# Linear attention beside softmax attention on one core: a transposing load held back, a copy split in two, the flag read earlier

## The chip, the core and the metric

The kernel runs on one core of one Trainium2 chip. The core has five engines with queues of their own: TensorE (PE, matrix products), VectorE (DVE), ScalarE (ACT), GpSimd (POOL) and SyncE (SP, which here only issues DMAs). Each works through its instructions in the order in which the program has them and waits on semaphores for the others. The metric is the device time of one execution in microseconds (us).

## The reference

Two attention blocks on inputs of their own, their results laid side by side. x is 1 x 2048 x 512, wqkv 512 x 1536, wo 512 x 512, all bfloat16; there are 32 heads of 16.

```python
def _A_ref(x, wqkv, wo):                      # linear attention
    q, k, v = qkv[0], qkv[1], qkv[2]          # qkv = x @ wqkv, split into heads
    phi = lambda t: jnp.where(t > 0, t + 1, jnp.exp(t)) + 1e-6
    pq, pk = phi(q), phi(k)
    kv = jnp.einsum("bhsd,bhse->bhde", pk, v)
    z = jnp.einsum("bhsd->bhd", pk)
    num = jnp.einsum("bhqd,bhde->bhqe", pq, kv)
    den = jnp.einsum("bhqd,bhd->bhq", pq, z)[..., None] + 1e-6
    o = num / den
    return (heads of o side by side) @ wo

def _B_ref(x, wqkv, wo):                      # softmax attention
    scores = jnp.einsum("bhqd,bhkd->bhqk", q, k) * Dh ** -0.5
    p = _softmax(scores, axis=-1)
    o = jnp.einsum("bhqk,bhkd->bhqd", p, v)
    return (heads of o side by side) @ wo

return jnp.concatenate([a, b], axis=-1)
```

Block B needs 32 x 2048 x 2048 exponentials, and these fill most of the time.

## The kernel before

**The work of B.** The 32 heads form four groups of eight, a group's 128 columns of Q and K being the 128 partitions of a tile. A unit of work is one group, 512 queries and one parity of heads; there are 32 units. Within a unit a block is 128 keys for one head: a matmul on 32 of TensorE's rows (L862) with the key tile KM, in which the other head of the 32 rows has been zeroed (L1366, L605), against the query tile QT. The scores lie in PSUM: five banks named pS, two of which or three are one ScalarE instruction (1024 or 1536 columns, L1074, to the tile PT), and two banks named pD for VectorE and GpSimd, which compute the exponential by integer arithmetic on the bits of a float16 (L978, L1148, tile DI). TensorE then multiplies by V, which carries a column of ones for the softmax sum (L1222, PSUM tile pPV). ScalarE's slots alternate: three banks, two banks, three banks.

**The order of the work.** The program plans itself while it is built: a loop keeps a time for each engine, a list of candidates and the times at which inputs are expected, and always takes the next candidate by its costs. What it takes becomes the fixed order of instructions of each engine. Work of block A, projections and outputs are jobs that are fitted in between. The planner begins only after a start that is written out by hand, with the engines' times and the due times of x's tiles set as constants. Semaphore waits follow from the reads and writes that each operation declares (`sch.add(lane, fn, reads, writes, queue=..., extra_deps=...)`); the first argument is the engine, or a DMA lane with a semaphore of its own, and `queue` is the engine that issues the DMA.

**The start.** B's x is wanted transposed, as the tile xTb with 16 tiles of 128 rows of x. Tiles 2 and 3 are loaded plainly (tile ON, ScalarE's queue) and transposed by TensorE (L1346); all others come by transposing DMAs on SP's queue (`load_t`, L443): tiles 0 and 1, 4 to 7, 8 to 11, 12 to 15. The weights are the tile Wb: ScalarE's queue loads the first 128 columns of K's and of Q's (keys ("Wb", 1, 0) and ("Wb", 0, 0)), SP's queue those of V (key ("Wb", 2)) behind tiles 4 to 7, and later the rest; A's x and weights (xTa, Wa) follow on SP. Then:

- `warm(n)` (L1335) issues n matmuls of 128 columns on a tile of zeros. WARM = (30, 8): 30 before the transposes of L1346, 8 behind them.
- `first_mm` (L1358) projects K of tile 0 (bank k0), Q of tiles 0 and 1 (q0), Q of tiles 2 and 3 (q1), K of tile 1 (k1), K of tiles 2 and 3 (k2). `first_ev` copies them to KM and QT: K by VectorE, twice with a mask; q0 by ScalarE (L1368), q1 by VectorE (L1370).
- The first five scores (L862) fill ScalarE's two slots. They wait for QT's pieces, keys ("QT0", 0) and ("QT0", 1).
- The planner's first jobs follow on TensorE in this order: K's projection for tiles 4 to 7 (L591), three scores for ScalarE's third exponential, V's projection (L668), two scores for the fourth exponential, V's projection again, and so on; K's projection for tiles 8 to 11 (L591) comes some rounds later.

**The end.** Four last stores go to the output (L1327). An operation "final" on GpSimd waits for the last store of every lane. Because the exponential is computed without subtracting the row's maximum, a bound on the scores is computed on the way (FLG); at the end each engine reads FLG into a register (L1594) and branches (L1596): where the bound is over a threshold, a general version of B runs instead. `emit_queue` writes an engine's instructions and calls `hook`, which holds this read, once it comes to an operation behind a given index, after that operation's waits. For GpSimd that operation is "final"; the other engines reach the end of their list and read there.

Of the kernel before, what the change touches and what calls it, by code (L numbers as in the profile page):

```python
# [238 lines left out]
def bass_concat_heads__linear_attn_block__softmax_full_mha__prompt_kernel(nc, A_x, A_wqkv, A_wo, B_x, B_wqkv, B_wo, out):  # L239
# [106 lines left out]
    DSH = 0.5  # L346
    FM = 0.06
    JB = True
    WARM = (30, 8)
    TRACE = None  # L350


# [3 lines left out]
    sch = Sched()  # L356
    es = contextlib.ExitStack()
    with es:
        block = es.enter_context(nc.Block())

        def sb(name, shape, dt):
            return es.enter_context(nc.sbuf_tensor(name, shape, dt))
# [4 lines left out]
        xTb = sb("xTb", [128, 4, S], BF)  # L367
        xTa = sb("xTa", [128, 2, 4, 512], BF)
        Wb = sb("Wb", [128, 4, 1536], BF)
        Wa = sb("Wa", [128, 4, 1536], BF)  # L370
        WOa, WOb = Wa[:, :, 512:1024], Wa[:, :, 1024:1536]
        QT = sb("QT", [128, 2, S], BF)
# [38 lines left out]
        def bank(T, b0, key):  # L411
            return (T, T.bitcast(BF), b0 * 512, key)
        DBANK = [bank(DB, i, ("D", i)) for i in range(NB)]
        SBANKS = [bank(S5, i, k_) for i, k_ in enumerate((("S", 0, 0), ("S", 0, 1), ("S", 0, 2), ("S", 1, 0), ("S", 1, 1)))]
# [10 lines left out]
        def gapped(ap, c0, n, run):  # L425

            base = ap[:, c0:c0 + run]
            return bass.AP(base.tensor, base.offset, [list(base.ap[0]), [run + 1, n], [1, run]])


        def load(dst_ap, src_ap, writes, queue="sp"):
            lane = sch.new_dma_lane()
            sch.add(lane, lambda e: e.dma_start(dst_ap, src_ap), writes=writes, queue=queue)
# [3 lines left out]
        on_keys = lambda k: [("ON", k, g) for g in range(8)] + ([("xTb", t) for t in range(4 * (k - 12), 4 * (k - 12) + 4)] if k >= 12 else [])  # L437
        on_at = lambda k: ONL[:, k, :] if k < 12 else xTb[:, 0, (k - 12) * 512:(k - 11) * 512]

        def load_t(dst, dname, x, t0, n):  # L440

            lane = sch.new_dma_lane()
            sch.add(lane, lambda e: e.dma_start_transpose(dst[:, :, t0 * 128:(t0 + n) * 128], x[0][t0 * 128:(t0 + n) * 128, :]),  # L443
                    writes=[(dname, t) for t in range(t0, t0 + n)], queue="sp")
        load(ONL[:, 2:4, :], B_x[0].rearrange("(t p) c -> p t c", p=128)[:, 2:4, :], on_keys(2) + on_keys(3), queue="act")
        load_t(xTb, "xTb", B_x, 0, 2)
        load(Wb[:, :, 512:640], wbv[:, :, 512:640], [("Wb", 1, 0)], queue="act")
        load(Wb[:, :, 0:128], wbv[:, :, 0:128], [("Wb", 0, 0)], queue="act")
        load_t(xTb, "xTb", B_x, 4, 4)
        load(Wb[:, :, 1024:1536], wbv[:, :, 1024:1536], [("Wb", 2)])  # L450
        load_t(xTb, "xTb", B_x, 8, 4)
        load_t(xTb, "xTb", B_x, 12, 4)
        load(Wb[:, :, 128:512], wbv[:, :, 128:512], [("Wb", 0, g) for g in range(1, NGP)])
# [76 lines left out]
        def push(eng, ready, prio, dur, run):  # L530
            seq[0] += 1
            c_ = (ready, prio, seq[0], dur, run)
            cands[eng].append(c_)
            return c_
# [282 lines left out]
        def unit(u):  # L817
            Gp, r2 = divmod(u, NC * 2)
            return (Gp,) + divmod(r2, 2)
# [45 lines left out]
        def qk_reads(bl):  # L865
            res = []
            for u, j, g in bl:
                Gp, c, e_ = unit(u)
                res += [("QT", Gp % 2, c), ("KMj", e_, j, g) if Gp % 2 == 0 and j < 4 else ("KM", Gp % 2, e_, j // 4, g)]
                if Gp == c == 0:  # L870
                    res += [("QT0", i) for i in range(2)]
            return res

        held = [False] * (NB + 1)
# [85 lines left out]
        def d_emit(tk, en):  # L960

            for b, buf, bi in tk:
                bk = DBANK[bi]
                sch.add("pe", lambda e, bk=bk, b=b: qk(e, f32v(bk), b), reads=qk_reads([b]), writes=[bk[3]])
            for b, buf, bi in tk:
                def p1(st_, en_, buf=buf, bi=bi):
                    bis = [bi]
                    for b2 in (bi + 1, bi - 1):
                        o = waiting.get(b2) if bi < NB and b2 < NB else None
                        if o is not None and o[0] == buf and o[2][0] <= st_ + 0.02:  # L970
                            cands["dve"].remove(o[2])
                            bis = sorted((bi, b2))
                            T["dve"] = en_ = st_ + 0.065 + 0.535 * 2
                            break
                    n, b0 = len(bis), bis[0]
                    s_ = dgroup["st"][buf]
                    i = len(s_["items"])
                    sch.add("dve", lambda e: e.tensor_scalar(DI[:, buf, D0_ + i * 512:D0_ + (i + n) * 512], f32v(DBANK[b0], n * 512),  # L978
                                                             ESC, EB, op0=ALU.mult, op1=ALU.add),
                            reads=[DBANK[x][3] for x in bis], writes=[("DI", 0, buf, i + x) for x in range(n)])  # L980
                    for x in bis:
                        b_ = waiting.pop(x)[1]
                        k_ = len(s_["items"])
                        s_["items"].append(b_)
                        dfree[x] = en_ + LPE["dve"]
                        pv_ready[b_[0]].append((en_ + LPE["dve"], b_, (DI.bitcast(F16)[:, buf, D0_ + k_ * 512:D0_ + (k_ + 1) * 512], ("DI", 0, buf, k_)), ("d", buf), "V"))
                    s_["t"] = en_
                    chain(buf)
                waiting[bi] = (buf, b, push("dve", en + LAT, 0, 0.6, p1))
# [16 lines left out]
        def fill_act_cand():  # L1006
# [24 lines left out]
            def run(st, en):  # L1031
# [28 lines left out]
                def f(e):  # L1060
                    for i, b in enumerate(bl):
                        ins = qk(e, S5[:, c0 + i * 512:c0 + (i + 1) * 512], b)
                    return ins
                sch.add("pe", f, reads=qk_reads(bl), writes=skeys(sl, len(bl)))
                if tk:
                    d_emit(tk, en + 0.05)
# [265 lines left out]
        def warm(n):  # L1332
            def f(e):
                for i_ in range(n):
                    ins = e.matmul(f32v(DBANK[0], 128), lhsT=ZW[:], rhs=ZW[:], start=True, stop=True)  # L1335
                return ins
            sch.add("pe", f, reads=["ZW"], writes=[DBANK[0][3]], accum="warm")
        warm(WARM[0])
        tok["Wb2"] = 10.9
# [3 lines left out]
        for t, bk, lane in ((2, SBANKS[1], "dve"), (3, SBANKS[2], "act")):  # L1343
            def tr(e, t=t, bk=bk):
# [6 lines left out]
                reads=[bk[3]], writes=[("xTb", t)])  # L1351
        warm(WARM[1])
        q0, q1, k0, k1, k2 = SBANKS[0], SBANKS[3], DBANK[2] if NB > 2 else SBANKS[4], DBANK[0], DBANK[1]

        def first_mm(bk, kind, t0, n, c0):
            def f(e):
                for cc in range(4):
                    ins = e.matmul(bk[0][:, bk[2] + c0:bk[2] + c0 + n * 128], lhsT=Wb[:, cc, kind * 512:kind * 512 + 128],  # L1358
                                   rhs=xTb[:, cc, t0 * 128:(t0 + n) * 128], start=(cc == 0), stop=(cc == 3))
                return ins  # L1360
            sch.add("pe", f, reads=[("Wb", kind, 0)] + [("xTb", t) for t in range(t0, t0 + n)], writes=[bk[3]])

        def first_ev(lane, bk, keys, dst, c0, n, wr, e_=None):
            src = bk[0][:, bk[2] + c0:bk[2] + c0 + n]
            if e_ is not None:
                sch.add(lane, lambda e: e.tensor_scalar(dst, src, PAR[:, e_:e_ + 1], None, op0=ALU.mult), reads=keys + [("PAR", e_)], writes=wr)  # L1366
            elif lane == "act":
                sch.add(lane, lambda e: e.activation(dst, src, ACTF.Copy), reads=keys, writes=wr)  # L1368
            else:
                sch.add(lane, lambda e: e.tensor_copy(dst, src), reads=keys, writes=wr)  # L1370
# [4 lines left out]
        for e_ in range(2):  # L1375
            first_ev("dve", k0, [k0[3]], KM[:, 0, e_, 0:128], 0, 128, kj(e_, [0]), e_)
        first_ev("act", q0, [q0[3]], QT[:, 0, 0:256], 0, 256, [("QT0", 0)])
        first_mm(q1, 0, 2, 2, 0)
        first_ev("dve", q1, [q1[3]], QT[:, 0, 256:512], 0, 256, [("QT0", 1)])
        first_mm(k1, 1, 1, 1, 0)  # L1380
        for e_ in range(2):
            first_ev("dve", k1, [k1[3]], KM[:, 0, e_, 128:256], 0, 128, kj(e_, [1]), e_)
# [108 lines left out]
        while True:  # L1491
# [5 lines left out]
            for eng in T:  # L1497
                best = None
                for c_ in cands[eng]:
                    st = max(T[eng], c_[0])  # L1500
                    k_ = (round(st / 0.05), c_[1], c_[2])
# [27 lines left out]
            t0 = min(o[0] for o in opts)  # L1529
# [41 lines left out]
        last = {}  # L1571
        for s_ in stores:
            last[s_.lane] = s_
        sch.add("pool", lambda e: None, extra_deps=list(last.values()), name="final")

        flag_op = sch.last_write["FLG"]
# [2 lines left out]
        sems = {ln: es.enter_context(nc.semaphore("s_" + ln)) for ln in sch.lane_ops.keys()}  # L1579
# [10 lines left out]
        def run(queue, e):  # L1590
            got = []
            def hook(e):
                e.wait_ge(sems[flag_op.lane], flag_op.count)
                got.append(e.value_load(FLG.bitcast(mybir.dt.int32)[0:1, 0:1], min_val=0))  # L1594
            sch.emit_queue(queue, e, sems, hook=(len(sch.ops) - 2, hook))
            with e.If(got[0] > THRESHOLD_BITS):  # L1596
                for ln, tot in totals.items():
                    if tot:
                        e.wait_ge(sems[ln], tot)
                gsch.emit_queue(queue, e, gsems)  # L1600
# [49 lines left out]
```

## Time and profile before

| what | us |
|---|---|
| median of 3 runs | 663.15 (663.01 to 664.05) |
| the profiled execution | 663.59 |
| its span, first to last instruction | 661.9 |
| ScalarE busy | 646.1 (98%) |
| TensorE busy | 635.4 (96%) |
| VectorE busy | 632.9 (96%) |
| GpSimd busy | 589.5 (89%) |

Rows of a timeline read: start in us, duration in us, engine, line, operation, output<-input, shapes, how many in a row; in brackets the engine's idle time before it and what ended it. PEld is TensorE's weight load ahead of a matmul, SPq and ACTq are the queues of SP and ScalarE with the DMAs that they issue. A row of DMA issues has the kilobytes of one and the us from its issue to its landing; where a stretch has only one such DMA, that is its own. A row of a DMA queue has packets, MB and the share of time of the 16 DMA engines. A row of one line's instructions has shortest, median and longest duration in ns and the first and last start in us.

### The profile page before, as it was taken

What the parts mean: (1) busy time and instruction counts of PE and PEld (TensorE: products, weight loads), DVE (VectorE), ACT (ScalarE), POOL (GpSimd) and SP (SyncE); (2) the same over time, 40 slices, a digit from 0 to 9 for tenths busy, and PEclk for the clock granted to TensorE, in tenths of its full rate; (3) what the DMA queues carried; (4) which work ended last, traced back from release to release, by engine and by line L of the source; (5) the groups of instructions that cost most, each with busy time, mean ns of one, the idle gap of its engine ahead of it and who ended that gap; (6) DMA issues with size and microseconds to landing.
All of it is one profiled execution on the core that took longest, in us unless ns stands there. A gap on an engine that the chain in (4) does not pass through costs nothing.

```text
span 661.9 us, 15921 instructions
## 1 busy us (share of the span) xinstructions
PE 635.4 (96%) x6603; PEld 201.5 (30%) x6658; DVE 632.9 (96%) x1065; ACT 646.1 (98%) x691; POOL 589.5 (89%) x493
## 2 busy tenths in 40 slices
PE   9999999999999999999999999999999999999996
PEld 6323332323323333323222223222222233222222
DVE  4999999999999999999999999999999999999985
ACT  6999999999999999999999999999999999999994
POOL 5989999998999998899989999899999999999981
PEclk9999999999999999999999999999999999999999
DMA  9701011010101101301002011100011000111011
GB/s 179 205 2 20 13 10 33 9 42 9 33 2 33 33 2 33 72 26 33 17 19 49 9 34 34 25 10 15 11 34 33 9 1 3 25 33 41 17 42 53
DMA packets 53214, 21.54 MB, mean 33 GB/s; under 512 B 44176, under 2 KB 52624, under 8 KB 53136
## 3 DMA queue, kind: packets, MB, share of 16 engines
q1 hardware_dynamic: 51664, 19.80, 13.4%
q8 instruction: 54, 0.88, 0.6%
q10 hardware_dynamic: 1472, 0.66, 0.4%
q14 instruction: 24, 0.20, 0.1%
HBM read 4.46 MB, written 4.19 MB: 13 GB/s over the span
## 4 chain that ended last, share of the span: by engine, by line
ACT 94%; PE 4%; DVE 1%; issue 0%; DMA 0%; DVEq 0%
ACT PT L1074 91%; ACT EA L684 2%; PE pD L800 1%; PE pPV L1222 1%; PE pS L862 1%; PE pD L1335 1%; DVE DI L978 0%; DMA out_dram<-KNa 0%; PE pS L1358 0%; DVE KNa L573 0%; PE pS L1274 0%; DVE DI L1154 0%; PE pS L800 0%; PE pS L1346 0%; PE pD L650 0%
## 5 line engine op out<-in xcount | busy, mean ns | idle before, releaser
L1074 ACT ACTIVATE PT<-pS 128x1024 f16<-128x1024 f32 (+1 forms) x653 | 639.0, 1312 | 1.0 <-PE pS L862 1.0
L1148 POOL TENSOR_SCALAR DI<-DI 128x1024 int16<-128x1024 int16 (+1 forms) x412 | 551.4, 1338 | 47.9 <-DVE DI L978 20.8
L978 DVE TENSOR_SCALAR DI<-pD 128x512 int16<-128x512 f32 (+1 forms) x463 | 324.5, 715 | 7.3 <-PE pD L862 3.9
L862 PE MATMUL pS<-QT,KM 32*128 32x512 bf16 x1555 | 256.8, 384 | 8.6 <-ACT PT L1074 3.4
L1222 PE MATMUL pPV<-PT,VV 128*17 128x512 f16 x1372 | 229.0, 381 | 0.0
L1222 PE MATMUL pPV<-DI,VV 128*17 128x512 f16 x1352 | 219.2, 381 | 0.2 <-DVE OT L1251 0.2
L862 PE MATMUL pD<-QT,KM 32*128 32x512 bf16 x493 | 168.7, 384 | 0.1
L1222 PE MATMUL pPV<-DI,VX 128*17 128x512 f16 x676 | 153.1, 384 | 0.0
L862 PEld LDWEIGHTS pS<-QT,KM 32*128 32x128 bf16 x1555 | 64.8, 90 | 263.7 <-ACT PT L1074 228.8
L978 DVE TENSOR_SCALAR DI<-pS 128x512 int16<-128x512 f32 x183 | 124.2, 679 | 1.1 <-PE pS L862 0.4
L1132 DVE TENSOR_SCALAR DI<-DI 128x1056 int16<-128x1056 int16 x118 | 80.6, 689 | 0.4
L1222 PEld LDWEIGHTS pPV<-PT,VV 128*17 128x17 bf16 x1372 | 47.7, 88 | 43.6 <-issue 37.8
L1222 PEld LDWEIGHTS pPV<-DI,VV 128*17 128x17 bf16 x1352 | 46.3, 88 | 40.6 <-issue 32.1
L862 PEld LDWEIGHTS pD<-QT,KM 32*128 32x128 bf16 x493 | 40.0, 91 | 5.2 <-DVE DI L978 2.5
L1222 PEld LDWEIGHTS pPV<-DI,VX 128*17 128x17 bf16 x676 | 32.8, 88 | 20.4 <-issue 17.0
L709 PE MATMUL pD<-Wa,xTa 128*128 128x256 bf16 x192 | 29.3, 275 | 0.0
L591 PE MATMUL pD<-xTb,Wb 128*128 128x512 bf16 x81 | 25.3, 382 | 3.3 <-issue 2.8
L1251 DVE STREAM_TRANSPOSE OT<-pPV 128x512 f32<-128x512 f32 x31 | 21.9, 707 | 0.1
L1257 POOL TENSOR_TENSOR OT<-OT,ZR 128x256 bf16<-128x256 f32 x31 | 19.2, 620 | 2.3 <-DVE ZR L1256 0.9
L684 ACT ACTIVATE EA<-pD 128x512 bf16<-128x512 f32 x22 | 18.6, 847 | 0.0
L709 PEld LDWEIGHTS pD<-Wa,xTa 128*128 128x128 bf16 x192 | 14.8, 97 | 12.5 <-issue 5.9
L573 DVE CAST KNa<-pD 128x512 bf16<-128x512 f32 x23 | 15.7, 682 | 2.1 <-PE pD L800 1.9
(145 smaller groups left out, 352.0 us busy)
## 6 DMA issues: line engine op xcount, KB each, us to landing
out_dram<-KNa SPq DMA_DIRECT2D x31, 128.0 KB, 1.7
Wa<-in_A_wqkv_dram SPq DMA_DIRECT2D x1, 1536.0 KB, 8.3
KM<-KR SPq DMA_DIRECT2D x96, 16.0 KB, 1.8
Wb<-in_B_wqkv_dram SPq DMA_DIRECT2D x2, 384.0 KB, 4.2
Wb<-in_B_wqkv_dram SPq DMA_DIRECT2D x1, 512.0 KB, 4.9
Wa<-in_A_wo_dram SPq DMA_DIRECT2D x1, 512.0 KB, 3.8
Wa<-in_B_wo_dram SPq DMA_DIRECT2D x1, 512.0 KB, 3.8
ON<-in_B_x_dram ACTq DMA_DIRECT2D x1, 256.0 KB, 2.8
```

What stands on the lines that cost most here:

```text
L573: return lambda e, bk: (e.tensor_copy(out_fn(), in_fn(bk)) if lane == "dve" else e.activation(out_fn(), in_fn(bk), ACTF.Copy))
L591: return e.matmul(f32v(bk), lhsT=Wb[:, cc, kind * 512 + Gp * 128:kind * 512 + Gp * 128 + 128], rhs=xTb[:, cc, sc * 512:(sc + 1) * 512], st ...
L684: ("act", 0.052 + n * 0.000833, f_ev("act", lambda e, bk: e.activation(EA[:, 0:n], f32v(bk)[:, c0:c0 + n], ACTF.Exp), [], ["EA"])),
L709: return e.matmul(f32v(bk)[:, 256 * tt:256 * tt + 256], lhsT=xTa[:, b, cc, (o + tt) * 128:(o + tt + 1) * 128], rhs=Wa[:, cc, 512 * kind + ...
L862: return e.matmul(dst, lhsT=KM[32 * g:32 * g + 32, Gp % 2, e_, j * 128:(j + 1) * 128], rhs=QT[32 * g:32 * g + 32, Gp % 2, c * 512:(c + 1) ...
L978: sch.add("dve", lambda e: e.tensor_scalar(DI[:, buf, D0_ + i * 512:D0_ + (i + n) * 512], f32v(DBANK[b0], n * 512), ESC, EB, op0=ALU.mult, ...
L1074: sch.add("act", lambda e: e.activation(PTf[:, p0 * 512:p0 * 512 + w], S5[:, c0:c0 + w], ACTF.Exp, scale=SC), reads=skeys(sl, len(bl)), wr ...
L1132: sch.add("dve", lambda e: e.tensor_scalar(gapped(DI[:, buf, :], DIV[v], wide // 32, 32), DI[:, buf, D0_ - 32:D0_ + w], 1.0, float(SHIFT[v ...
L1148: sch.add("pool", lambda e: e.tensor_scalar(DI[:, sl, DIV[v]:DIV[v] + w], DI[:, sl, D0_:D0_ + w], 1.0, float(SHIFT[v - 1]), op0=ALU.mult, ...
L1222: sch.add("pe", lambda e, g=g, j=j, c0=c0, V_=V_, r2=r2, P=P, first=first, last_=last_: e.matmul(PVb[32 * g:32 * g + 17, 0:512] if len(P.s ...
L1251: sch.add("dve", lambda e: e.transpose(OT[:, 0, :], PVb[:, 0:512]), reads=[("PV", g) for g in range(4)], writes=[("OT", 0)])
L1257: ("pool", 0.7, f_op("pool", lambda e: e.tensor_tensor(xn[:, :, 16 * e_:16 * e_ + 16], o[:, :, 0:16], zr.unsqueeze(2).broadcast_to([128, 1 ...
```

## The change

- `load_t` takes a list of keys, and the DMA for tiles 4 to 7 waits until ("Wb", 0, 0), Q's first 128 columns of weights, has landed. The wait stands in SP's queue.
- The 8 matmuls of the second `warm` become 4.
- The projection of Q for tiles 2 and 3 becomes two, each with a bank of its own and 128 columns: VectorE copies tile 2's, ScalarE tile 3's. The first scores wait for three pieces of QT instead of two.
- An operation "mark" on GpSimd, which does nothing, stands ahead of "final", and `hook` is set to come ahead of it. GpSimd so reads FLG before it waits for the stores; the branch stays behind that wait. The other engines read it where they did.

The planner's constants stay as they are, and so does the order of everything behind the first projections.

```diff
-    WARM = (30, 8)
+    WARM = (30, 4)
...
-        def load_t(dst, dname, x, t0, n):
+        def load_t(dst, dname, x, t0, n, after=()):
 
             lane = sch.new_dma_lane()
             sch.add(lane, lambda e: e.dma_start_transpose(dst[:, :, t0 * 128:(t0 + n) * 128], x[0][t0 * 128:(t0 + n) * 128, :]),
-                    writes=[(dname, t) for t in range(t0, t0 + n)], queue="sp")
+                    writes=[(dname, t) for t in range(t0, t0 + n)], queue="sp", extra_deps=[sch.last_write[k_] for k_ in after])
...
-        load_t(xTb, "xTb", B_x, 4, 4)
+        load_t(xTb, "xTb", B_x, 4, 4, [("Wb", 0, 0)])
...
-                    res += [("QT0", i) for i in range(2)]
+                    res += [("QT0", i) for i in range(3)]
...
-        first_mm(q1, 0, 2, 2, 0)
-        first_ev("dve", q1, [q1[3]], QT[:, 0, 256:512], 0, 256, [("QT0", 1)])
+        q2 = SBANKS[1]
+        first_mm(q1, 0, 2, 1, 0)
+        first_mm(q2, 0, 3, 1, 0)
+        first_ev("dve", q1, [q1[3]], QT[:, 0, 256:384], 0, 128, [("QT0", 1)])
+        first_ev("act", q2, [q2[3]], QT[:, 0, 384:512], 0, 128, [("QT0", 2)])
...
+        mark = sch.add("pool", lambda e: None, name="mark")
         sch.add("pool", lambda e: None, extra_deps=list(last.values()), name="final")
...
-            sch.emit_queue(queue, e, sems, hook=(len(sch.ops) - 2, hook))
+            sch.emit_queue(queue, e, sems, hook=(mark.idx - 1, hook))
```

## The prediction

> **What bounds the kernel now.** I read the page first: the chain that ended last, then the costliest groups.
>
> ```profile
> ACT 94%; PE 4%; DVE 1%; issue 0%; DMA 0%; DVEq 0%
> L1074 ACT ACTIVATE PT<-pS 128x1024 f16<-128x1024 f32 (+1 forms) x653 | 639.0, 1312 | 1.0 <-PE pS L862 1.0
> ```
>
> ScalarE's exponentials are the kernel: 94% of the chain, and ahead of all 653 together ScalarE idled 1.0 us. So a delay that reaches this stream early is not made up later, and the only time to be won lies before its first exponential and behind its last. The chain in order of time shows the start:
>
> ```profile
> 1.06 3.38 PE pD L1335 x30
> ...
> 5.29 0.85 PE pD L1335 x8
> 6.14 1.51 PE pS L1358 x12
> 7.65 0.66 PE pD L1358 x8
> ...
> 8.68 3.71 ACT PT L1074 x3
> ```
>
> TensorE is in the chain from 1.06 us on, first with the dummy matmuls of L1335 (eight of them just before the first projections, L1358), and ScalarE starts at 8.68. The third view is SP's own queue in the timeline, which is where the change puts its wait, with the landing times of what was issued (last column, us from issue).
>
> ```profile
> 0.81 1.35 SPq L443 DMA_TRANSPOSE xTb<-in_B_x_dram  x1
> 2.22 3.60 SPq L443 DMA_TRANSPOSE xTb<-in_B_x_dram  x1
> 5.87 0.59 SPq L433 DMA_DIRECT2D Wb<-in_B_wqkv_dram  x1
> 6.51 4.05 SPq L443 DMA_TRANSPOSE xTb<-in_B_x_dram  x1
> ```
> ```profile
> L433 ACTq DMA_DIRECT2D Wb<-in_B_wqkv_dram x2: 488/508/528, 1.3 to 1.8; - x2
> ```
> ```profile
> Wb<-in_B_wqkv_dram ACTq DMA_DIRECT2D x1, 128.0 KB, 4.5
> xTb<-in_B_x_dram SPq DMA_TRANSPOSE x1, 5.1
> xTb<-in_B_x_dram SPq DMA_TRANSPOSE x1, 5.7
> Wb<-in_B_wqkv_dram SPq DMA_DIRECT2D x1, 512.0 KB, 4.9
> xTb<-in_B_x_dram SPq DMA_TRANSPOSE x1, 8.4
> ```
>
> In order of issue these five are Q's first weights (1.8 + 4.5 = 6.3), x's tiles 0 and 1 (5.9), tiles 4 to 7 (2.22 + 5.7 = 7.9), V's weights (5.87 + 4.9 = 10.8), tiles 8 to 11 (6.51 + 8.4 = 14.9). SP issues without a gap: a transposing DMA holds its queue for up to 4.05 us. Who needs them is in TensorE's weight loads, and what ScalarE does meanwhile in its timeline:
>
> ```profile
> 8.24 0.28 PEld L862 LDWEIGHTS pS<-QT,KM 32*128 32x128 bf16 x5 [0.21 <-DVE QT L1370]
> ```
> ```profile
> 8.98 0.55 PEld L591 LDWEIGHTS pD<-xTb,Wb 128*128 128x128 bf16 x4
> ...
> 10.18 0.10 PEld L862 LDWEIGHTS pS<-QT,KM 32*128 32x128 bf16 x3
> ...
> 11.04 0.45 PEld L668 LDWEIGHTS pD<-Wb,xTb 128*128 128x128 bf16 x8 [0.22 <-issue]
> 11.59 0.09 PEld L862 LDWEIGHTS pS<-QT,KM 32*128 32x128 bf16 x2
> 11.91 0.45 PEld L668 LDWEIGHTS pD<-Wb,xTb 128*128 128x128 bf16 x8 [0.23 <-issue]
> ...
> 15.09 0.11 PEld L591 LDWEIGHTS pD<-xTb,Wb 128*128 128x128 bf16 x2 [0.29 <-DVE VV L672]
> ```
> ```profile
> 10.93 1.46 ACT L1074 ACTIVATE PT<-pS 128x1536 f16<-128x1536 f32 x1
> ```
> ```profile
> 12.26 1.04 ACT L1074 ACTIVATE PT<-pS 128x1024 f16<-128x1024 f32 x1
> ```
>
> L591 at 8.98 reads tiles 4 to 7, with 1.1 us in hand; L668 at 11.04 reads V's weights, with 0.2 us in hand; L591 at 15.09 reads tiles 8 to 11, with 0.2 us. TensorE works in order, and behind each of the first two stand the scores (L862) of ScalarE's third and fourth exponential, at 10.93 and 12.26.
>
> **The hold on tiles 4 to 7.** SP now waits for Q's weights before it issues them, and everything behind on SP waits too: V's weights, tiles 8 to 15, the rest of Wb, and A's inputs. When do Q's weights land, if tiles 4 to 7 don't travel beside them? Packets by queue in two stretches, 4.0 to 4.8 us and 4.8 to 5.9 us (q10 is ScalarE's queue with the weights, q1 SP's):
>
> ```profile
> q10 hardware_dynamic: 727, 0.18, 107.9%
> q1 hardware_dynamic: 139, 0.03, 17.3%
> ```
> ```profile
> q1 hardware_dynamic: 582, 0.15, 98.8%
> q10 hardware_dynamic: 215, 0.05, 30.0%
> ```
>
> The last 215 packets of the weights took 1.1 us beside SP's; at the earlier 727 in 0.8 us they take 0.24, so up to 0.8 us is won: a landing between 5.5 and 6.3. I take 5.6, as SP's packets had little else than tiles 4 to 7 in them. The Trainium skill, "DMA: Bandwidth & Descriptors" (Queues, rings and completion order), has a reason why it could be earlier: the semaphore's write lands only after all earlier writes of that DMA engine, those of other queues too. The trace agrees as far as tiles 0 and 1 go, which land at 5.9 though q1 went almost quiet after 4.0; by that rule an estimate of 5.4 would come out for the weights and the sum would be 0.2 us lower.
>
> Then the DMA itself. The same shape and size (four tiles) with nothing before it in its queue is in A's loads, and a 512 KB load behind such a one is Wo's:
>
> ```profile
> L460 SPq DMA_TRANSPOSE xTa<-in_A_x_dram x12: 1303/2335/3837, 15.6 to 386.7; - x12
> ...
> DMA to landing us min/median/max: 4.3/4.4/7.0
> ```
> ```profile
> Wa<-in_A_wo_dram SPq DMA_DIRECT2D x1, 512.0 KB, 3.8
> ```
>
> Issue: 1.30 to 3.60 (as now); I take the median 2.34, since the queue is empty by then. Landing: 4.3 to 5.7, taken 4.4. V's weights: 3.8 (nothing behind them) to 4.9 (now, with tiles 8 to 11 issued right behind, which stays so), taken 4.9. With 0.05 us between issues as now:
> - tiles 4 to 7 issued at 5.65, landed at 10.05 (2.1 later than now). L591 goes from 8.98 to 10.1, the scores behind it 1.20 later (8.98 to 10.18), ScalarE 0.44 after these (8.24 to 8.68): third exponential at 11.74, 0.8 late.
> - V's weights issued at 8.05, landed at 12.95. L668 at 13.0, scores at + 0.55 (11.04 to 11.59), ScalarE + 0.44: fourth exponential at 13.99, 1.73 late. This one decides; the third alone would give 11.74 + 1.33 = 13.07.
> - From there TensorE needs 0.87 us a round (11.04 to 11.91) against ScalarE's 0.9 to 1.33, so the 1.73 neither grows nor shrinks. Next to be late are tiles 8 to 11: 2.2 later, 17.1, against 15.09 + 1.73 = 16.8. Two exponentials are then queued ahead of TensorE, which covers 0.3; without that cover it would be paid in full. The other inputs move by 2.2 us too; the first to be used are A's:
>
> ```profile
> L709 PEld LDWEIGHTS pD<-Wa,xTa x192: 95/98/99, 42.0 to 272.6; 128*128 128x128 bf16 x192
> ```
>
> Issued by 23 us now, they keep ample room. Bounds of this part: +0.6 (5.5, 1.30, 4.3, 3.8: the third exponential at 11.54 decides) to +3.7 (6.3, 3.60, 4.9: V's weights at 14.9).
>
> **Four dummy matmuls fewer, Q's columns split.** Four of L1335's eight are 0.43 us, so the first projection could start at 5.5 instead of 6.0 if its inputs land earlier too. The split costs ScalarE one copy and shortens VectorE's:
>
> ```profile
> 7.69 0.42 DVE L1370 CAST QT<-pS 128x256 bf16<-128x256 f32 x1 [0.43 <-PE pS L1358]
> ```
> ```profile
> L1368 ACT ACTIVATE QT<-pS 128x256 bf16<-128x256 f32 x1 | 0.4, 383 | 1.3 <-PE pS L1358 1.3
> ```
>
> ScalarE's copy takes at most 0.38 and lies in the 1.0 us in which ScalarE waited before 8.68; the scores waited 0.21 for VectorE's. Matmul columns are the same. Together the first exponential comes 0 to 0.6 earlier, but the third waits for tiles 4 to 7, so I count 0. Only if the hold were free would these 0.6 be worth anything.
>
> **The flag.** GpSimd read the flag after the last store had landed; now before. The end:
>
> ```profile
> L1594 POOLq TENSOR_LOAD <-FLG x1: 496/496/496, 660.7 to 660.7; - x1
> ```
> ```profile
> L1596 POOLq COMPARE_BRANCH  x1: 53/53/53, 661.4 to 661.4; - x1
> ```
> ```profile
> L358 ACTq DRAIN  x1: 99/99/99, 660.8 to 660.8; - x1
> L358 POOLq DRAIN  x1: 50/50/50, 661.6 to 661.6; - x1
> ```
>
> From 660.7 to 661.4 goes, 0.7 us. ScalarE's drain at 660.8 is next and leaves 0.1 above it, so I count 0.65 (0.4 to 0.7).
>
> **Sum.** +1.73 - 0.65 = +1.08 us. The profiled execution (663.59, span 661.9) becomes 664.67; it stood 0.44 above the median of 663.15, which becomes 664.2. Some 0.2%, 1.33 us, is about what a measurement of this kernel can tell from no change; this is within it.
>
> **Rivals.**
> - *SP's queue pays in full* (the other side: slower). It decides once V's weights land after 13.2, where loss less 0.65 passes 1.33. At the upper bounds, issue 3.60 as now and weights at 6.3, they land at 14.9: +3.7 - 0.65, 666.2. For it: every transposing DMA of the first 15 us but the half-size one held SP for 3.6 us or more. Against it: those stood in a full queue. 0.20, anywhere from 664.5 up.
> - *The hold is nearly covered.* V's weights in 3.8 us as Wo's, issue 1.3 to 1.8: the third exponential decides, +0.6, and 663.1 results. Against it: tiles 8 to 11 follow right behind. 0.16.
> - *The loss is not carried to the end*, or the start is won: -0.65 alone gives 662.5, with 0.6 of start 661.9. Against it the 1.0 us of idle in the whole stream. 0.08.
> - *TensorE falls back to its slow rate.* It idles about 1.4 us before 10.1 and 1.1 before 13.0. The first matmuls of the chain run at 0.11 us for 128 columns, against 0.66 us for 1536 columns from 7.65 on, so half rate exists here. Rounds of 0.87 then become about 1.5 against ScalarE's mean 1.12: 0.6 at the fourth exponential and 0.4 in each of three rounds, 666.0. 0.08. The Trainium skill, "TensorE: Matmul & The Clock Gate" (Part 1), lets the rate fall only after a whole idle window of some 3.4 us, longer than either gap; no run shown here tests it.
>
> **How the numbers follow.** Forecast 0.48, its own range 663.6 to 665.2 (loss of 1.1 to 2.7); the others as above. Over 664.48 lies a good third of the forecast (0.17), the first rival 0.18 and the slow rate 0.08: slower 0.43. Faster than 661.8 only the very end of the third rival: 0.03. The rest, 0.54, is no change. The range is 662.4 to 666.2, which leaves out the won start and the worst of both slow cases.
>
> **What would show it.** SP's second transposing DMA starts near 5.65 and lasts 2.3; V's weights land near 13; L591 waits until 10.1 and L668 until 13.0, each for a DMA; ScalarE idles before its third and fourth exponential, 1.7 us later at the fourth than at 12.26, and hardly after that; GpSimd's flag load stands before 655. Wrong would be: no ScalarE idle there, a queue time of 3.6, matmuls of L668 at twice their spacing, or an end that ScalarE's drain holds.

## The result, and the profile after

The changed kernel takes 665.93 us (median of five runs, 665.28 to 667.89); the kernel before, run beside it, 663.44 (663.01 to 664.05). The ratio is 1.0044, with a 95% interval from 1.0032 to 1.0055: slower by 2.5 us, where 1.08 was forecast. The interval does not hold 1, so this is more than scatter. The profiled execution took 665.88, with a span of 664.1 (before: 661.9).

The page of the changed kernel, the shares of the chain that ended last and the group of the exponentials:

```profile
ACT 93%; PE 4%; DMA 2%; SPq 0%; DVE 0%; issue 0%; ACTq 0%; DVEq 0%
...
L1074 ACT ACTIVATE PT<-pS 128x1024 f16<-128x1024 f32 (+1 forms) x653 | 639.2, 1308 | 2.6 <-PE pS L862 2.6
```

DMA is in the chain now, and ScalarE's idle time ahead of the exponentials went from 1.0 to 2.6 us. SP's queue in the timeline of the changed kernel (start, duration):

```profile
5.99 2.41 SPq L443 DMA_TRANSPOSE xTb<-in_B_x_dram  x1
...
8.45 0.59 SPq L433 DMA_DIRECT2D Wb<-in_B_wqkv_dram  x1
```

V's weights in its DMA issues from 8 to 9 us (last column: us from issue to landing):

```profile
Wb<-in_B_wqkv_dram SPq DMA_DIRECT2D x1, 512.0 KB, 4.4
```

The hold lasts to 5.99, the transposing DMA holds SP for 2.41, V's weights are issued at 8.45 instead of 5.87 and land at 12.9. TensorE's weight loads and ScalarE's timeline of the changed kernel show who waits:

```profile
10.52 0.56 PEld L591 LDWEIGHTS pD<-xTb,Wb 128*128 128x128 bf16 x4 [2.10 <-issue]
...
12.97 0.46 PEld L668 LDWEIGHTS pD<-Wb,xTb 128*128 128x128 bf16 x8 [0.62 <-issue]
13.54 0.09 PEld L862 LDWEIGHTS pS<-QT,KM 32*128 32x128 bf16 x2
```
```profile
8.24 2.37 ACT L1074 ACTIVATE PT<-pS 128x1536 f16<-128x1536 f32 x2 [0.72 <-PE pS L862]
12.15 1.45 ACT L1074 ACTIVATE PT<-pS 128x1536 f16<-128x1536 f32 x1 [1.54 <-PE pS L862]
13.97 6.95 ACT L1074 ACTIVATE PT<-pS 128x1024 f16<-128x1024 f32 x7 [0.37 <-PE pS L862]
```

The first exponential is 0.44 earlier (8.24), the third 1.22 later (12.15), the fourth 1.71 later (13.97). ScalarE's last instruction in the timelines, of before and then of after:

```profile
655.95 0.59 ACT L573 ACTIVATE KNa<-pS 128x512 bf16<-128x512 f32 x1
```
```profile
657.64 0.59 ACT L573 ACTIVATE KNa<-pS 128x512 bf16<-128x512 f32 x1
```

It is 1.69 later, so the 1.71 was carried through the whole kernel. The rest of the loss is behind this instruction. First before, where ScalarE branches at 657.7 (its drain stood at 660.8) and the last store, issued at 657.18, takes 3.5 us to land; then after, with the branches (L1600), the flag loads (L1598), the drains and the last store:

```profile
L1596 ACTq COMPARE_BRANCH  x1: 54/54/54, 657.7 to 657.7; - x1
```
```profile
out_dram<-KNa SPq DMA_DIRECT2D x1, 128.0 KB, 3.5
```
```profile
L1600 ACTq COMPARE_BRANCH  x1: 54/54/54, 659.7 to 659.7; - x1
L1600 POOLq COMPARE_BRANCH  x1: 53/53/53, 663.4 to 663.4; - x1
```
```profile
L1598 POOLq TENSOR_LOAD <-FLG x1: 486/486/486, 655.2 to 655.2; - x1
```
```profile
L358 POOLq DRAIN  x1: 45/45/45, 663.5 to 663.5; - x1
L358 ACTq DRAIN  x1: 80/80/80, 663.8 to 663.8; - x1
```
```profile
658.88 1.19 SPq L1327 DMA_DIRECT2D out_dram<-KNa  x1
```
```profile
out_dram<-KNa SPq DMA_DIRECT2D x1, 128.0 KB, 4.5
```

GpSimd's flag load is out of the way at 655.2, and its branch follows the landing of the last store (658.88 + 4.5) at once. But that landing takes 1.0 us longer than before, and ScalarE's way from branch to drain 4.1 us instead of 3.1; ScalarE's drain is now the last. From the start of ScalarE's last instruction to the end of the span it was 5.9 us (655.95 to 661.9) and is 6.5 (657.64 to 664.1): 0.6 more, where 0.65 less was forecast.

So two questions: what lengthened the end, and whether the 1.7 us of the start is what an execution usually loses.

### The profile page after: what moved, and what is told of

The parts are those of the page before. It is cut to its first block, busy times and chain, and to the rows that moved or that the text cites. A ratio compares the mean times of both kernels' runs of the same rounds, so it can differ in the third digit from the quotient of the medians.

```text
span 664.1 us, 15976 instructions
## 1 busy us (share of the span) xinstructions
PE 643.7 (97%) x6658; PEld 201.1 (30%) x6658; DVE 632.8 (95%) x1065; ACT 646.6 (97%) x692; POOL 589.6 (89%) x493
## 4 chain that ended last, share of the span: by engine, by line
ACT 93%; PE 4%; DMA 2%; SPq 0%; DVE 0%; issue 0%; ACTq 0%; DVEq 0%
ACT PT L1074 90%; ACT EA L684 2%; DMA Wb<-in_B_wqkv_dram 1%; PE pPV L1222 1%; PE pS L862 1%; PE pD L800 1%; SPq L443 0%; DMA out_dram<-KNa 0%; DVE KNa L573 0%; PE pS L1274 0%; PE pS L800 0%; ACTq L433 0%; PE pD L650 0%; PE pD L668 0%; PE pPV L1483 0%
## 5 line engine op out<-in xcount | busy, mean ns | idle before, releaser
L591 PE MATMUL pD<-xTb,Wb 128*128 128x512 bf16 x100 | 29.5, 384 | 2.3 <-DMA xTb<-in_B_x_dram 1.9
L675 POOL TENSOR_SCALAR VX<-VV 128x544 bf16<-128x544 bf16 x16 | 10.3, 644 | 8.5 <-DVE VV L672 7.5
```

The source lines that it names most:

```text
L591: return e.matmul(f32v(bk), lhsT=Wb[:, cc, kind * 512 + Gp * 128:kind * 512 + Gp * 128 + 128], rhs=xTb[:, cc, sc * 512:(sc + 1) * 512], st ...
L675: st.append(("pool", 0.7, f_op("pool", lambda e: e.tensor_scalar(VX[:, r, 4 * t4:4 * t4 + 4, :].rearrange("p t c -> p (t c)"), VV[:, r, 4 ...
```

## The experiments

Theories at the outset: the hold costs about 1.7 us through V's weights (H); the flag read early is worth 0.65 (F); and, for the end, that ScalarE's one copy more lengthens its way from branch to drain (A), against the rival that the start's other changes or the hold itself did it. All times below are medians with range and number of runs; the kernel before, beside them, had 663.41 to 663.54. "Tail" is the time from the start of ScalarE's last instruction to the end of the span in the profiled execution.

**Hold alone.** Before, with the `after=` of `load_t` and the list of keys for tiles 4 to 7.

```diff
-        load_t(xTb, "xTb", B_x, 4, 4)
+        load_t(xTb, "xTb", B_x, 4, 4, [("Wb", 0, 0)])
```

> The kernel before with the hold on tiles 4 to 7 alone. Theory 1 (the hold's loss is taken at ScalarE's fourth exponential, as in the trace of the changed kernel, where it starts at 13.97 instead of 12.26, and is carried to the end unchanged; what the changed kernel lost beyond this lies at its end and comes from the flag): +1.7 us on the kernel before, fourth exponential near 14.0, last stores landing 3.5 us after their issue as before. Theory 2 (the hold also spoils the end, or the end varies by chance whatever the edit): +2.2 to +3.0 us, with a last store that takes 4.5 us and ScalarE's drain about 4 us behind its branch.

Measured: 665.77 (665.22 to 667.4, 5), ratio 1.0039 (1.0025 to 1.0052): +2.3 us, the time of theory 2 without its end: the tail is 5.6 us, not longer than before, and the last store lands 3.2 us after its issue, so the hold doesn't touch the end. The fourth exponential starts at 14.79, later than the 13.97 of the changed kernel, although V's weights land 0.2 us earlier than there. The reason is in the windows of this kernel, cut at the 3.41 us in which the granted clock changes (columns: busy time of TensorE, its weight loads, VectorE, ScalarE, GpSimd with counts; granted clock of TensorE as a share of its full rate; DMA share; GB/s):

```profile
3.90:7.32 3.42, 2.76 (x40) 2.51 (x38) 1.27 (x4) 0.98 (x2) 3.42 (x8) 1.00 0.42 82
7.32:10.73 3.41, 1.55 (x12) 0.60 (x10) 1.49 (x5) 2.36 (x2) 1.34 (x6) 1.00 0.98 187
10.73:14.14 3.41, 3.41 (x17) 1.34 (x16) 1.41 (x2) 1.44 (x1) 0.00 (x0) 0.50 1.12 284
```

TensorE, which waits for tiles 4 to 7, is busy for 1.55 of 3.41 us, and in the next stretch it is granted half its clock: 17 matmuls fill it entirely. In the changed kernel the fourth exponential started 1.10 us after V's weights had landed (12.87, 13.97); here that would be 13.76, so the half clock cost 1.0 us. The same view of the changed kernel's execution shows no fall:

```profile
9.41:12.82 3.41, 2.09 (x12) 0.79 (x12) 1.21 (x2) 1.87 (x3) 0.00 (x0) 1.00 0.99 234
12.82:16.23 3.41, 3.23 (x40) 2.16 (x40) 0.89 (x2) 3.04 (x4) 0.64 (x1) 1.00 1.17 142
```

There the stretches begin at another time, the idle time is divided between two of them, and none holds less than 2.09 us of work. So the forecast's rival "TensorE falls back to its slow rate" is real in some executions.

**Flag alone.** Before, with `mark` and the hook ahead of it.

```diff
+        mark = sch.add("pool", lambda e: None, name="mark")
...
+            sch.emit_queue(queue, e, sems, hook=(mark.idx - 1, hook))
```

> The kernel before with the flag read ahead of the stores' wait alone. Theory 1 of the forecast: -0.65 us, GpSimd's drain at 660.9 beside ScalarE's. Rival, by the changed kernel's trace: reading early lengthens the end (ScalarE's drain 4.1 us behind its branch instead of 3.1, last store 4.5 us instead of 3.5), so +0.3 to +1.0 us. Third: the end varies by chance, then -0.65 us in some runs and up to +0.5 in others, with a wider spread than before's 1 us.

Measured: 662.99 (662.63 to 663.15, 11), ratio 0.9991 (0.9982 to 1.0000): -0.46 us, with an upper end of the interval at no change. The tail is 5.1 us, 0.8 less than before's. This is the fastest kernel of the study.

**The changed kernel without the hold**, and **the start without hold and flag** (four dummy matmuls fewer and the split of Q's columns, on the kernel before).

> The changed kernel without the hold: four dummy matmuls fewer, the split copy and the early flag. If the hold is the loss: no idle before the third and fourth exponential, first exponential 0.2 to 0.4 earlier than 8.68 and all of it carried to the end, with the flag's 0.65 in all -0.8 to -1.1 us on the kernel before (662.4 to 662.6). If the early flag costs at the end: -0.4 + 0.3 to 1.0, thus 0 to +0.6 us.

> Four dummy matmuls fewer and the split copy, nothing else. Theory 1: the first exponential starts at 8.2 to 8.5 instead of 8.68 and the rest follows: -0.2 to -0.45 us. Rival (the tiles and weights land where they did and TensorE only waits for them): 0 to -0.2 us from the split alone. Rival (the dummy matmuls are missed: TensorE reaches its full rate later): +0.1 to +0.5 us, with the first scores later than 8.24.

Measured: without the hold 664.06 (663.72 to 665.11, 11), 1.07 over the flag alone; the start alone 664.30 (663.98 to 665.32, 11), ratio 1.0014 (1.0005 to 1.0023), 0.85 over before, more than any of the three theories gave. The first exponentials are where they were (8.78 in the start alone), so the loss isn't in the start: its tail is 7.0 us. Something of the start's edits lengthens the end.

**One ScalarE instruction more, otherwise nothing.** Before, with L483, a 4-element activation, written twice. The two run at 3.65 and 3.89 us, while ScalarE's first work comes at 5.33.

```diff
         sch.add("act", lambda e: e.activation(DUM[:, 4:8], DUM[:, 0:4], ACTF.Exp), reads=[("ZR", 0)], writes=[("ZR", 0)])
+        sch.add("act", lambda e: e.activation(DUM[:, 4:8], DUM[:, 0:4], ACTF.Exp), reads=[("ZR", 0)], writes=[("ZR", 0)])
```

> The kernel before with the four-element activation of the start issued twice: one more instruction in ScalarE's queue, in time that ScalarE idles (0.2 us). Theory A (the split's cost at the end comes from the one instruction more: in the three kernels with the split ScalarE's drain comes 3.5 to 4.6 us behind its branch, in the three without it 2.7 to 3.1): drain 3.5 to 4.6 us behind the branch here too and an end held by ScalarE, +0.3 to +0.9 us on the kernel before. Theory B (the split's cost is in the start or is chance): drain about 3 us behind the branch and 0 us (within 0.2).

Measured: 664.38 (663.64 to 665.34, 11), ratio 1.0015 (1.0007 to 1.0024): +0.97 us for an instruction that does nothing and delays nothing. Its branch and drains (lines are one further down):

```profile
L1597 ACTq COMPARE_BRANCH  x1: 54/54/54, 658.2 to 658.2; - x1
```
```profile
L358 ACTq DRAIN  x1: 80/80/80, 661.8 to 661.8; - x1
L358 POOLq DRAIN  x1: 50/50/50, 662.4 to 662.4; - x1
```

From branch to drain ScalarE takes 3.6 us against 3.1, its branch stands 0.3 later behind its last instruction than before, and the last store lands 4.2 us after its issue. The end isn't held by ScalarE, as the expectation had it, but by GpSimd, which waits for that store; in the start alone ScalarE's drain is the last (662.7, GpSimd's 661.9). Both ways to the end get longer. The split's cost is thus the mere presence of its copy. But is it the number of instructions, or where they lie?

**Six more**, the same line seven times in all. They run from 3.9 to 5.3 us, not before 2 as expected, and still end before ScalarE's first work at 5.33.

> The kernel before with six more 4-element activations on ScalarE at the start, behind the one that is there; they run before 2 us, long before ScalarE has anything to do. Theory A1 (the end is longer by a step: one more fetch of instructions behind the last exponential, whatever the number): ScalarE's way from its branch to its drain is 3.5 to 4.6 us as with one extra, and the time is 664.0 to 664.8 (+0.6 to +1.4). Theory A2 (each extra instruction lengthens it): +0.97 x 6, about 669. Rival (act_extra's +0.97 was a matter of runs): 663.2 to 663.7, branch to drain 2.7 to 3.1.

Measured: 663.38 (662.89 to 663.91, 11), ratio 0.9998 (0.9989 to 1.0007). Both theories fall: no step that stays, no cost for each. Branch and drain:

```profile
L1602 ACTq COMPARE_BRANCH  x1: 54/54/54, 657.7 to 657.7; - x1
```
```profile
L358 ACTq DRAIN  x1: 81/81/81, 660.6 to 660.6; - x1
```

2.9 us. The DMA queue that fetches instructions in pieces of 8 KB (q14), first from 655.0 to 657.6 and then from 657.7 to 664.5:

```profile
q14 instruction: 1, 0.01, 1.0%
...
q14 instruction: 5, 0.04, 2.1%
```

The same second stretch of the kernel with one instruction more, which has no such packet in the first:

```profile
q14 instruction: 6, 0.05, 2.7%
```

Before has five in the second stretch and none in the first. So with one instruction more there is one fetch more behind ScalarE's branch; with six more it stands ahead of the branch (656.55), beside ScalarE's last work, and the time is that of before. That the packet is ScalarE's is inferred from its time; the queue doesn't say.

**Controls.** The memset of L482 on VectorE twice; and the four dummy matmuls fewer alone.

> The kernel before with the 4-element memset of L482 twice, so one more instruction on VectorE at the start and none on ScalarE. Theory A (only the engine whose drain holds the end matters, and that is ScalarE): 663.2 to 663.7, the time of before, and ScalarE's way from branch to drain stays at 2.7 to 3.1 us. Rival (any instruction more anywhere moves code and costs): +0.8 to +1.0, 664.3.

> The kernel before with four dummy matmuls fewer, nothing else. Theory A (start_only's +0.85 is all from ScalarE's one copy more): 663.2 to 663.7, no difference, the first exponential where it was, since TensorE then waits for tiles 0 and 1. Rival (the fewer dummy matmuls cost, through a slower first projection): 664.0 or more, with the first exponential at 9.1 or later.

Measured: 663.46 (663.09 to 664.05, 11), ratio 1.0000; and 663.50 (663.25 to 663.84, 11), ratio 1.0000. An instruction more on VectorE costs nothing, and the four dummy matmuls neither cost nor gain anything: with them gone TensorE waits for x's tiles 0 and 1 (0.47 us in this kernel, 0.20 in the changed one).

**Both of the split's copies on VectorE**, in the changed kernel, so that ScalarE has as many instructions as before.

```diff
-        first_ev("act", q2, [q2[3]], QT[:, 0, 384:512], 0, 128, [("QT0", 2)])
+        first_ev("dve", q2, [q2[3]], QT[:, 0, 384:512], 0, 128, [("QT0", 2)])
```

> The changed kernel with both halves of the split copy on VectorE, so that ScalarE's queue has as many instructions as before. Theory A: ScalarE's drain 2.7 to 3.1 us behind its branch and the flag's gain there: 0.5 to 1.2 us faster than the changed kernel, that is +1.2 to +2.0 us on the kernel before, of which the hold's wait is +1.7 in runs where TensorE keeps its rate. Theory B: as the changed kernel, +2.5 us.

Measured: 665.62, the median of nine (eight from 664.43 to 669.81, one at 1797.94), ratio 1.0033 (1.0016 to 1.0050). That is +2.2, over the +1.2 to +2.0 of theory A, and with this spread the time alone doesn't decide. The profiled execution, of 669.6, does for the end: its tail is only 5.1 us. Its ScalarE is yet 6.8 us late at its last instruction, since TensorE was granted half its clock from 11.65 to 25.30.

**The changed kernel with five ScalarE instructions more**, six with the split's copy, beside **the changed kernel once more**.

> The changed kernel with five more 4-element activations on ScalarE at the start, so that with the split's copy it has six instructions more than before, as the kernel with six extra ones had. Theory P (what the split cost lies in where the boundaries of the fetched pieces of ScalarE's instructions fall: one instruction more puts a fetch behind the branch, six put it ahead): ScalarE's way from branch to drain is 2.7 to 3.1 us instead of 4.15, a fetch of instructions stands between 656 and 659, and the time falls by 0.5 to 1.0 below that of the changed kernel run beside it, to 664.9 to 665.5. Rival (the copy costs by itself, in the start): no difference to the changed kernel, branch to drain 3.5 to 4.6. Either way the hold's loss stays: not below 664.5.

> The changed kernel once more, for comparison on the same chip and for its spread: 665.3 to 667.9, median 665.9. In the profiled execution the time to the fourth exponential is 13.9 to 14.1 where TensorE's rate rises at 6 us or later, and 14.6 to 15.4 where it rises before 5 us and so falls again between 10.6 and 11.7.

Measured: 665.22 (664.41 to 666.8, 6) against 666.26 (665.51 to 668.25, 5): 1.04 us less by five instructions more. The ratios' intervals, 1.0015 to 1.0040 and 1.0025 to 1.0053, overlap; the end of the profile is plainer. With the five:

```profile
L1605 ACTq COMPARE_BRANCH  x1: 54/54/54, 660.2 to 660.2; - x1
```
```profile
L358 ACTq DRAIN  x1: 81/81/81, 663.2 to 663.2; - x1
L358 POOLq DRAIN  x1: 45/45/45, 663.2 to 663.2; - x1
```

3.0 us from branch to drain, and a tail of 5.0 against 6.0 in the repeated kernel. The fetch that was expected ahead of the branch is there, from 656 to 660 the only one of 8 KB (it starts at 659.0):

```profile
q14 instruction: 1, 0.01, 0.8%
```

The tails of all profiled executions together:

| ScalarE's instructions | flag read late | flag read early |
|---|---|---|
| as before, or six more | 5.6 to 5.9 (before, hold alone, dummy matmuls alone, VectorE's extra, six extra, hold with busy TensorE) | 5.0 to 5.1 (flag alone, copies on VectorE, the changed kernel with five more) |
| one more | 6.4 to 7.0 (start alone, one extra, the changed kernel with the late flag) | 5.9 to 6.5 (the changed kernel twice, without hold, V's weights on ScalarE's queue) |

Down a column the copy costs about 0.9 to 1.0, along a row the flag wins about 0.6, and the two add up. The landing of the last store goes with it: 3.2 to 3.5 us after issue in the upper row, 3.8 to 4.5 in the lower. Two more marks divide these 16 traces in the same way. Behind ScalarE's branch stand five fetches of 8 KB in all nine of the upper row and six in all seven of the lower (the last of them up to 0.5 us past the span's end). And from the end of ScalarE's flag load to its branch it takes 0.16 us in the upper row and 0.44 to 0.45 in the lower. This second mark is ScalarE's own, which makes it likely that the sixth fetch is too.

The repeated kernel's profiled execution is its slowest, 668.25. Its windows:

```profile
8.69:12.10 3.41, 1.70 (x10) 0.70 (x11) 0.64 (x1) 1.83 (x3) 0.27 (x2) 1.00 1.38 252
12.10:15.51 3.41, 2.43 (x18) 1.32 (x16) 0.77 (x2) 1.55 (x2) 0.00 (x0) 0.50 1.08 163
15.51:18.93 3.42, 3.42 (x27) 2.15 (x26) 0.69 (x1) 2.88 (x3) 0.65 (x1) 0.50 0.91 133
```

1.70 us of work in the first, half the clock in the next two, the fourth exponential at 15.31 and ScalarE's last instruction 4.6 us later than before. V's projections come 1.51 us apart, where the changed kernel's first execution had 0.89 (12.97 to 13.86):

```profile
13.69 0.77 PEld L668 LDWEIGHTS pD<-Wb,xTb 128*128 128x128 bf16 x8 [1.44 <-DVE KM L605]
...
15.20 0.77 PEld L668 LDWEIGHTS pD<-Wb,xTb 128*128 128x128 bf16 x8 [0.44 <-issue]
```

Its rate had risen at 5.28, in the gap that the expectation left between "before 5" and "at 6 or later", and the fall came at 12.1, outside the 10.6 to 11.7 written there.

**The flag read late in the changed kernel.**

> The changed kernel with the flag read where it was (hold, fewer dummy matmuls and the split stay). Theory A (with the copy more on ScalarE its drain is the last thing, so the early flag wins little): 665.9 to 666.3, at most 0.4 above the changed kernel. Rival (the flag is worth its 0.5 to 0.7 whatever else is there): 666.5 or more. GpSimd's drain would come 0.5 to 0.7 after the changed kernel's, beside or behind ScalarE's.

Measured: 666.69 (665.97 to 670.58, 6), ratio 1.0057 (1.0037 to 1.0078), over 666.5 as the rival had it; part of it is a fall of the clock in some executions (the profiled one too, from 10.68 to 14.10). By the table the flag keeps about 0.6 beside the copy, though the ranges of that row touch (6.4 to 7.0, 5.9 to 6.5). In this profile GpSimd's drain stands 0.5 behind ScalarE's (664.7, 664.2), so reading late does hold the end. This speaks against the theory A of this expectation; the times alone, 0.4 to 0.8 over the changed kernel's two medians, wouldn't settle it.

**What the hold costs: TensorE kept busy.** Hold alone, with 28 dummy matmuls ahead of L591, so that TensorE isn't idle while it waits for tiles 4 to 7.

```diff
+                        for i_ in range(28):
+                            ins = e.matmul(f32v(bk, 128), lhsT=ZW[:], rhs=ZW[:], start=True, stop=True)
```

> The hold alone, with 28 dummy matmuls of 128 columns on TensorE just before the projection that waits for tiles 4 to 7, so that TensorE does not idle about 2 us there. Theory C (TensorE's rate falls to half in some executions because of this idle time, as in the profile of the hold alone, where the granted clock is 0.50 from 10.7 to 14.1 us and the fourth exponential starts at 14.79): no stretch at 0.50 after the start, fourth exponential at 13.8 to 14.1, +1.5 to +1.9 us on the kernel before, and runs within 1 us of each other instead of 2.2. Rival (the spread of the runs has nothing to do with the rate): +2.3 us and a spread of 2 us as with the hold alone.

Measured: 666.19 (665.48 to 668.45, 6), not faster than the hold alone, and with a spread of 3 us where theory C wanted 1. The clock doesn't fall in its profile, and yet the fourth exponential starts at 14.65, because V's weights landed only at 13.55 (1.10 us before, as in the changed kernel): in its DMA issues they take 5.7 us.

```profile
Wb<-in_B_wqkv_dram SPq DMA_DIRECT2D x1, 512.0 KB, 5.7
```

So the slow rate isn't the whole of what the forecast left out; the landing of V's weights is the other part. The mean granted clock of each execution fits: in the hold alone it is 0.999 at 665.22 and 665.45, 0.996 at 665.77 and 666.0, 0.993 at 667.4. (It also counts the fall behind the last matmul, and is 0.996 in the start alone with no other; lower values tell of a fall before.) Here it is 0.993 at 668.45, so the rate fell in one execution in spite of the dummy matmuls. But one execution of the changed kernel took 667.89 at 0.999: a fallen rate doesn't explain that one.

**V's weights past SP.** The changed kernel with V's weights on ScalarE's queue, ahead of the hold.

```diff
-        load(Wb[:, :, 1024:1536], wbv[:, :, 1024:1536], [("Wb", 2)])
+        load(Wb[:, :, 1024:1536], wbv[:, :, 1024:1536], [("Wb", 2)], queue="act")
```

> The changed kernel with V's weights issued by ScalarE's queue, so that they do not stand behind the hold; tiles 4 to 7 still do. If V's place behind the hold decides, as in the forecast: the fourth exponential follows the third without a wait, the third is late by 0.8 to 1.2 us, and the whole is 0.5 to 1.2 us faster than the changed kernel (+1.3 to +2.0 us on the kernel before). If V's weights, now beside Q's, slow these down: tiles 4 to 7 are held longer and land after 10.4, and the whole is no faster than the changed kernel.

Measured: 667.5 (665.57 to 668.02, 5), ratio 1.0062 (1.0049 to 1.0075). V's weights land at 7.50, but tiles 4 to 7, beside them, only at 11.11, and the third exponential goes to 12.85. The wait changes its place and stays. Its profiled execution is the fastest of the five. It has the least work in a stretch of any that kept its clock:

```profile
9.81:13.22 3.41, 1.75 (x11) 0.79 (x12) 0.91 (x2) 1.37 (x3) 0.00 (x0) 1.00 1.44 189
```

## Why the prediction was wrong

**What held.** That ScalarE bounds the kernel and that a delay at its start is carried: 1.71 us at the fourth exponential, 1.69 at its last instruction. The path through SP's queue, in the profiled execution: tiles 4 to 7 issued in 2.41 us (2.34 taken), landed after 4.4 (4.4 taken), V's weights landed at 12.9 (12.95), the fourth exponential at 13.97 (13.99). That it decides, and not the third. Its meeting the forecast to 0.02 is luck in part: the hold lasted 0.34 longer than taken (5.99 against 5.65; 5.81 to 5.99 in seven traces), so that the third exponential was 1.22 late instead of 0.8, and V's weights landed 4.4 after their issue instead of 4.9. The flag: 0.46 in the medians, about 0.6 in the tails (0.65 taken, 0.4 to 0.7 allowed). The dummy matmuls: nothing. The first exponential 0.44 earlier without use.

**What failed first: the split costed at nothing.** "ScalarE's copy takes at most 0.38 and lies in the 1.0 us in which ScalarE waited": true of its time of execution, and it missed that a copy is also an instruction in ScalarE's stream. It cost 0.85 us with the dummy matmuls beside it, 0.97 as an empty instruction, and about 1.0 in the changed kernel by the five that took it away again (there the intervals overlap). The forecast had named "an end that ScalarE's drain holds" as what would make it wrong, but took 0.1 us of distance for enough and asked only how far the drain was, not whether the change could move it. With the copy's 0.9 to 1.0 the profiled execution's sum is 1.69 - 0.6 + 0.9 to 1.0 = 2.0 to 2.1, against the 2.3 between the two spans.

**What failed second: the hold's size in the usual execution.** The median of the hold alone is +2.3, not +1.73. Of the seven profiled executions with the hold in SP's queue ahead of V's weights, the changed kernel's was the luckiest: ScalarE's last instruction is 1.7, 2.4, 2.5, 2.6, 2.6, 4.6 and 6.8 us later than before. Two causes, each seen alone: V's weights land anywhere from 12.66 to 13.66 (4.4 to 5.8 us after their issue, with 4.9 taken), which cost 0.7 at the fourth exponential in the hold with busy TensorE (14.65 against the changed kernel's 13.97); and TensorE's rate falls in five of the seven, which cost 1.0 there in the hold alone. Where it stays half for one stretch of 3.41 us (three of them), that and the landing together make 2.5 to 2.6; for two and four stretches 4.6 and 6.8. The rival of the slow rate had the right mechanism, and rounds of about 1.5 us, as measured (1.51); its 0.08 was too low. That its 666.0 lies beside the 665.93 measured is luck: it stood for a hold of 3.5 us (1.73 + 1.8) and a free copy, and the profiled execution of the changed kernel kept its rate. The rate fell after stretches of 3.41 us with 1.31 to 1.70 us of work, and didn't after 1.75 and 2.09. The Trainium skill's rule in "TensorE: Matmul & The Clock Gate" (Part 1), of a whole idle window, had spoken against this rival; these traces disagree with it.

**The sum, by the runs.** Hold 2.32, copy 0.85 to 0.97, dummy matmuls 0, flag -0.46: 2.7 to 2.8, against 2.49 and 2.82 measured in two comparisons of the changed kernel. With the copy's place in the stream mended: 2.32 - 0.46 = 1.86, against 1.78. The time lies in the range given, close to its upper end, but by other terms than those that had set this bound (the issue at 3.60 did not occur).

**What stays open.** Why the landing of V's weights differs by a us between executions of the same order: where they were issued earlier (7.8 to 7.9) they mostly landed later (12.9 to 13.7) than where issued at 8.2 and 8.5 (12.7 and 12.9), which no run isolates. What made the execution of 667.89 long. Whose the sixth fetch is, and why the last store lands later along with it. The Trainium skill, "DMA: Bandwidth & Descriptors" (Queues, rings and completion order), lets a semaphore's write wait for earlier writes of the same DMA engine, those of other queues too, which would fit a fetch in its way; no run here shows it by itself.

## What to carry to other kernels

An edit on the engine that bounds the kernel isn't free because its time is hidden: code is still fetched behind the last work, and here one instruction more on ScalarE lengthened the end by about a us, where six more didn't. So such an edit should be measured beside the same count of empty instructions. A wait that is added ahead of a queue also idles TensorE, and here 1.7 us of idleness in a stretch of 3.41 was enough to lose its rate; the price then hangs on where the stretch begins, and shows as spread between runs before it shows in one profile. The part of a change that takes work off the end (here the flag, 662.99) can be kept alone.

## What the runs showed of the hardware

- An activation of four elements that delays nothing cost 0.97 us (one more), and six of them nothing. Behind ScalarE's branch stood six fetches of 8 KB with the one, five without it and with the six. So the number isn't what counts; that it is the position in the stream of fetches is inferred.
- The granted clock of TensorE fell to 0.50 after stretches of 3.41 us in which it had worked for 1.31, 1.45, 1.55, 1.56 and 1.70 us, and kept its rate after 1.75, 2.09 and more. It stayed at half for 3.41, 6.83 or 13.65 us, and the stretches began at another time in each execution.
- A transposing DMA of four tiles of x held SP for 1.8 to 2.4 us where SP had waited before it, and for 2.0 to 4.9 (mostly 3.5 and more) behind other loads of the queue. The load of 512 KB behind the first took 4.4 to 5.8 us to land with the same work around it.
